# A mixer kernel on one core: the remainders and the root in the loop of the second norms

## The chip, the core and the metric

The kernel runs on one core of a Trainium2 chip. The core has five engines with an instruction queue each: TensorE (PE in the profile, with its weight loads as PEld) for matrix products, VectorE (DVE), ScalarE (ACT) and GpSimd (POOL) for elementwise work, and SyncE (SP), which issues DMAs. Each engine works through its own queue in order, and engines wait for each other by semaphores. The metric is the device time of one execution in microseconds (us): the median of several runs.

## The reference

`x` is 2048 tokens of 640 channels. Two blocks follow each other, each behind a layer norm whose scale and shift come from a conditioning vector, and each added to `x` through a gate:

```python
mod = (silu(c) @ w_mod).reshape(1, 6, 1, 640)      # sa, ca, ga, sb, cb, gb
h = layernorm(x) * (1 + ca) + sa
x = x + ga * A(h, k, v, shift_k, ssm_k, ssm_D)      # causal convolutions, gated by h
h = layernorm(x) * (1 + cb) + sb
x = x + gb * B(h, w1, b1, w2, b2)                   # token mixing

def B(x, w1, b1, w2, b2):
    h = layernorm(x)                                # a second norm, over the channels again
    u = gelu(einsum("bsd,sf->bdf", h, w1) + b1)     # F = 1728
    return (einsum("bdf,fs->bds", u, w2) + b2).transpose(0, 2, 1)
```

So between the two blocks each token's row is normalized, scaled and shifted by `1 + cb` and `sb`, and normalized once more. The change lies in the loop that does this second normalization and feeds the first product of block B.

## The kernel before

The first 300 us compute block A with Fourier matrices on TensorE. From about 300 us on, the kernel takes the 2048 tokens as 16 row tiles `j` of 128 tokens by 640 channels, two at a time: pair `pr` holds the tiles `2*pr` and `2*pr + 1`, pairs 0 to 7. `row(j)` is a tile's work place in SBUF; for tiles 4 and up it is the tile of `x` itself.

Products are made in fp32r, and so each factor is split into a half (the value rounded to fp32r) and a remainder (value minus half): three products, half by half, half by remainder and remainder by half, stand for one. `H[j]` is the pair (half, remainder) of the normalized row; `blk[f]` the pair for the weights of block `f`, of 128 columns of `w1`. The first four blocks of weights (f = 0 to 3) are multiplied inside the loop, pair by pair, and accumulate in four PSUM tiles `acc`; the other ten follow after the loop (from L882) with all 16 rows at once.

The steps for one pair:

- `x1_stats` (L665): VectorE ends the statistics of the first norm of a row (`bn_stats` L510, `bn_aggr` L668).
- `norm1` (L704): ScalarE applies the first norm to the two rows (L706).
- `second` (L708): VectorE multiplies both rows by `1 + cb` and sums them (L712), makes the negative mean (L714) and adds it and `sb` (L717); ScalarE squares each row and sums the squares into a column of `V_` (L722). The squares' own values go to the place of the later remainder and are not used.
- `root_in` (L683): the root's bias. GpSimd turns the sum of squares into a variance plus epsilon (L688) and does the same for the first norm of a pair that comes later (L691); ScalarE takes the square root of these few columns (L692).
- `root` (L694): VectorE makes the reciprocal root from it in four small operations (`newton`, L318 to L321), and the first norm's bias (L701). The result is `R_`.
- `halves` (L724): ScalarE writes the halves, `row * R_` rounded (L726).
- `rests` (L728): VectorE writes the remainders, `row * R_ - half` (L730), one instruction per row.
- `products` (L733): TensorE, 48 matmuls per pair (L433): for each row and each of the four blocks the half with the weights' half and with the weights' remainder, then for each row the remainder with the weights' half. For the last pair all three steps of a block come together.

The weights of the blocks are split by rows, four tiles `j` at a time (`split_rows`, L406): the halves on ScalarE (L409), the remainders on VectorE (L411, recorded under the helper's line L59). In the loop, `split_rows` for tiles 8 to 11 gives its halves in turn 3 and its remainders in turn 4, and for tiles 12 to 15 in turns 5 and 6.

Nothing is planned by a scheduler: the kernel asks for a manual schedule, and each engine's queue holds its instructions in the order in which the Python program writes them. That order is a matter of latency as well as of work: in the loop (L795 to L812) the queue of VectorE holds, per turn, `second` of this pair, the remainders of the pair before, in turns 4 and 6 the weight remainders, the statistics for a pair that comes later, and then the root. `root_in` comes between the statistics and the root. TensorE's products of the pair before stand behind the remainders. In turn 4, at its end, SyncE is given the load of the next block of weights (`load_w(4)`) into the tile `X`, whose old contents the weight remainders of that turn read last.

Of the kernel before, what the change touches and what calls it, by code (L numbers as in the profile page):

```python
# [10 lines left out]
F32R = mybir.dt.float32r  # L11
AF = mybir.ActivationFunctionType
ALU = mybir.AluOpType
# [36 lines left out]
def mixer_kernel(ctx: ExitStack, tc: tile.TileContext, q, k, v, shift_k, ssm_k, ssm_D, w1, b1, w2, b2, c,  # L50
# [7 lines left out]
    act, dve, pool, pe, sync = nc.scalar, nc.vector, nc.gpsimd, nc.tensor, nc.sync  # L58
    TT = lambda eng, o, a, b, op: eng.tensor_tensor(o, a, b, op=op)  # L59
    uid = [0]  # L60

    def mem(tag, n, name=None):

        return sb.tile([128, n], F32, name=name or tag, tag=tag, bufs=1)
# [4 lines left out]
    def psum(slot=None):  # L69

        uid[0] += 1
        slot = ring[uid[0] % len(ring)] if slot is None else slot
        return psp.tile([128, 1024], F32, name=f"pst_{uid[0]}", tag=f"pst{slot}", bufs=1)
# [242 lines left out]
    def newton(r, t, v, n=None):  # L316

        dve.reciprocal(r, t)  # L318
        dve.scalar_tensor_tensor(t, r, -0.5, r, op0=ALU.mult, op1=ALU.mult)
        TT(dve, t, t, v, ALU.mult)  # L320
        dve.scalar_tensor_tensor(r, t, 1.5, r, op0=ALU.add, op1=ALU.mult)  # L321
# [64 lines left out]
    def load_w(i, t=X):  # L386
        if i >= NF + NW:
            return
        if i < NF:
            t = j16(t)  # L390
            for b in range(2):
                sync.dma_start(t[64 * b:64 * b + 64],
                               dram(w1, 16 * b * F + fo(i), [[32 * F, 64], [F, 16], [1, 128]]))
            raw[i] = (t, [slice(0, 8), slice(8, 16)])
        else:
            t = f14(t)
            load_w2(t, i - NF, 0, 14)
            raw[i] = (t, [slice(0, 7), slice(7, 14)])
# [7 lines left out]
    def split_rows(r, t, blocks, hi=True, lo=True):  # L406
        j, t = slice(4 * r, 4 * r + 4), t.rearrange("p (j m) -> p j m", j=4)
        for f in blocks if hi else ():
            act.activation(blk[f][0][:, j].bitcast(F32R), t[:, :, 128 * f:128 * f + 128], AF.Copy)  # L409
        for f in blocks if lo else ():  # L410
            TT(dve, blk[f][1][:, j].bitcast(F32R), t[:, :, 128 * f:128 * f + 128], blk[f][0][:, j], ALU.subtract)  # L411
# [15 lines left out]
    def mm(ps, wh, wl, rh, rl, first, last, steps=None):  # L427

        m = wh.shape[-1]
        steps = steps or ((wh, rh), (wh, rl), (wl, rh))  # L430
        for i, (w_, r_) in enumerate(steps):
            for h in range(2):
                pe.matmul(ps[0:m, h, 0:320], w_.bitcast(F32R), r_[:, 320 * h:320 * h + 320].bitcast(F32R),  # L433
                          start=first and i == 0, stop=last and i == 2)
# [76 lines left out]
    for c in range(NC):  # L511
# [141 lines left out]
        else:  # L653
# [5 lines left out]
    H = (unit(r_z[:, 0:4096], 3) + unit(r_v, 3) + unit(mem("aux", 4096, "h_a"), 3)  # L659
         + unit(r_z[:, 3840:7680], 3))  # L660
    tmp = piece(mem("g", 1280, "t_g"), 2) + piece(T_t, 2)
    row = lambda j: tmp[j] if j < 4 else XR(j)
    acc = []

    def x1_stats(js):  # L665
        for j in js:
            x1s(NC - 1, j)()
            dve.bn_aggr(mv[:, j, :], bst[:, j])  # L668


    V_, T_, R_ = (T_kt[:, o:o + 32] for o in (1280, 1312, 1344))
# [9 lines left out]
    at = lambda t, n, j: t[:, place[n, j]:place[n, j] + 1]  # L681

    def root_in(n):  # L683

        second_, first_ = roots[n]
        o = start[n]
        if second_:
            pool.tensor_scalar(V_[:, o:o + 2], V_[:, o:o + 2], 1 / D, EPS, op0=ALU.mult, op1=ALU.add)  # L688
            o += 2
        if first_:  # L690
            pool.tensor_scalar(V_[:, o:start[n + 1]], mv[:, first_[0]:first_[-1] + 1, 1], EPS, None, op0=ALU.add)  # L691
        act.activation(T_[:, start[n]:start[n + 1]], V_[:, start[n]:start[n + 1]], AF.Sqrt)  # L692

    def root(n):  # L694

        o = slice(start[n], start[n + 1])
        newton(R_[:, o], T_[:, o], V_[:, o])
        first_ = roots[n][1]
        if first_:
            f = slice(first_[0], first_[-1] + 1)  # L700
            dve.scalar_tensor_tensor(nm1[:, f], mv[:, f, 0], -1.0, R_[:, start[n + 1] - len(first_):start[n + 1]],  # L701
                                     op0=ALU.mult, op1=ALU.mult)

    def norm1(pr):  # L704
        for j in (2 * pr, 2 * pr + 1):
            act.activation(row(j), XR(j), AF.Identity, scale=at(R_, 1, j), bias=nm1[:, j:j + 1])  # L706

    def second(pr):  # L708

        for j in (2 * pr, 2 * pr + 1):  # L710
            t = row(j)
            dve.scalar_tensor_tensor(t, t, 1.0, CB, op0=ALU.mult, op1=ALU.mult, accum_out=su[:, j:j + 1])  # L712
        n = su[:, 2 * pr:2 * pr + 2]
        dve.tensor_scalar(n, n, msb, -1 / D, op0=ALU.add, op1=ALU.mult)  # L714
        for j in (2 * pr, 2 * pr + 1):
            t = row(j)
            dve.scalar_tensor_tensor(t, t, su[:, j:j + 1], SB, op0=ALU.add, op1=ALU.add)  # L717
        for j in (2 * pr, 2 * pr + 1):
            if j == 12:
                H.extend(unit(mem("xa", 5120, "h_x"), 4))  # L720
            H[j] = H[j][:, 0:640], H[j][:, 640:1280]
            act.activation(H[j][1].bitcast(F32R), row(j), AF.Square, accum_out=at(V_, 2, j))  # L722

    def halves(pr):  # L724
        for j in (2 * pr, 2 * pr + 1):
            act.activation(H[j][0].bitcast(F32R), row(j), AF.Identity, scale=at(R_, 2, j))  # L726

    def rests(pr):  # L728
        for j in (2 * pr, 2 * pr + 1):
            dve.scalar_tensor_tensor(H[j][1].bitcast(F32R), row(j), at(R_, 2, j), H[j][0], op0=ALU.mult,  # L730
                                     op1=ALU.subtract)

    def products(pr, fs=range(4)):  # L733
        for f_ in fs:
            if f_ == len(acc):
                acc.append(psum().rearrange("p (h m) -> p h m", h=2))
        js = [(f_, j) for j in (2 * pr, 2 * pr + 1) for f_ in fs]
        if pr == 7:
            for f_, j in sorted(js):
                mm(acc[f_], blk[f_][0][:, j], blk[f_][1][:, j], *H[j], False, j == 15)  # L740
            return
        for rest in range(2):
            for f_, j in js:
                wh, wl = blk[f_][0][:, j], blk[f_][1][:, j]
                mm(acc[f_], wh, wl, *H[j], j == 0 and not rest, False, ((wh, H[j][1]),) if rest else
                   ((wh, H[j][0]), (wl, H[j][0])))
# [28 lines left out]
    halves(0)  # L775
    norm1(1)
    rests(0)
    products(0, range(3))
    x1_stats(range(4, 6))
    second(1)  # L780
    gate(NC - 1, ps, 1, dve, then=(lambda: root_in(2), lambda: root(2), lambda: halves(1), lambda: norm1(2)))
    spill(NC - 1, (1,))
    products(0, [3])
    rests(1)
    products(1)
    second(2)
# [3 lines left out]
    halves(2)  # L790
    norm1(3)
    rests(2)
    norm1(4)
    products(2)
    for pr in range(3, 8):  # L795
        second(pr)
        if pr > 3:
            rests(pr - 1)
            products(pr - 1)
        if pr in (4, 6):  # L800
            split_rows(pr // 2, X if pr == 4 else P, range(4), False, True)
        if pr < 6:
            x1_stats(range(2 * pr + 4, 2 * pr + 6))
        root_in(pr + 1)
        root(pr + 1)
        halves(pr)
        if pr < 6:
            norm1(pr + 2)
        if pr in (3, 5):
            split_rows(pr // 2 + 1, X if pr == 3 else P, range(4), True, False)  # L810
        if pr == 4:
            load_w(4)  # L812
# [258 lines left out]
def build(inputs):  # L1071
    import concourse.bacc as bacc

    nc = bacc.Bacc("TRN2", target_bir_lowering=False, num_devices=1)
    arrays, args = {}, []

    def add(name, a):
        a = np.ascontiguousarray(a)
        arrays[f"in_{name}_dram"] = a
        args.append(nc.dram_tensor(f"in_{name}_dram", a.shape, mybir.dt.from_np(a.dtype), kind="ExternalInput").ap())  # L1080

    for name in _INS:
        a = np.asarray(inputs[name])
        add(name, a.reshape(S, D) if name in ('A_q', 'A_k', 'A_v') else a)
    for name, a in _constants().items():
        add("const_" + name, a)
    args.append(nc.dram_tensor("out_0_dram", (S, D), F32, kind="ExternalOutput").ap())
    with tile.TileContext(nc) as tc:
        mixer_kernel(tc, *args)
    return nc, arrays  # L1090
# [8 lines left out]
```

## Time and profile before

| what | value |
| --- | --- |
| three runs, median | 702.24 us |
| three runs, lowest to highest | 700.96 to 708.29 us |
| the profiled execution | 707.76 us |
| its span, first to last instruction | 706.0 us |
| mean granted clock of TensorE | 0.977 |
| busy in the span: PE, DVE, ACT, POOL | 624.8, 485.5, 293.0, 128.3 us |

The profile is of one execution, with the start and the duration of each instruction. A row of the lists in order of time gives the start in us, the duration in us, the engine, the line of the kernel, the operation, output and inputs by the program's names, shapes, and the number of like instructions that the row merges; in square brackets stand the idle time of the engine ahead of it and what ended that. Where a row merges two instructions, its duration runs from the first one's start to the last one's end. L59 is a helper's line, for all two-operand operations of VectorE and GpSimd. `wb` is a tile of split weights, `h_a`, `r_z`, `r_v` and `h_x` are tiles that hold `H`, `xa` and `xb` hold the rows, `kt` holds the few columns of the root, `p` and `x` the raw weights, and `m_p`, `m_v`, `m_w` belong to the last stage.

### The profile page before, as it was taken

Reading aid. Unit: us, or ns where it says so; the run is one execution under the profiler, and the core shown is the slowest. Engines: PE = TensorE matmul, PEld = TensorE weight load, DVE = VectorE, ACT = ScalarE, POOL = GpSimd, SP = SyncE. Lnnn points to the kernel's source line nnn. Section 1 sums busy time; section 2 is a strip of 40 time slices with the busy share of each in tenths; the row PEclk is TensorE's granted clock in tenths of the full one; section 3 lists DMA queues with packets and bytes.
Section 4 is the critical chain, followed back from the end, with each engine's and each line's share of the span. In section 5 each row is a group of like instructions: output and inputs, shape, how many; then the busy total and the mean of one; then the engine's idle time right before and its main releaser. Section 6 shows DMA issues by size and latency. Waiting matters only on the chain.

```text
span 706.0 us, 20772 instructions
## 1 busy us (share of the span) xinstructions
PE 624.8 (89%) x9131; PEld 603.1 (85%) x9131; DVE 485.5 (69%) x849; ACT 293.0 (42%) x465; POOL 128.3 (18%) x147
## 2 busy tenths in 40 slices
PE   0698576898999988888799999999999998999997
PEld 0698266888998878778799999999999998999997
DVE  7779338987979539888885213211399959888986
ACT  0444263554746636456666223222335223333331
POOL 5183018512524125000110000000000340000000
PEclk9999888999999999999999999999999999999999
DMA  9977988617343524161303633353163343455411
GB/s 185 248 216 214 368 174 175 149 32 162 71 90 91 172 63 119 58 151 31 59 1 60 118 63 61 75 103 62 53 193 105 106 140 110 145 170 170 148 60 38
DMA packets 167185, 84.91 MB, mean 120 GB/s; under 512 B 89235, under 2 KB 157622, under 8 KB 167094
## 3 DMA queue, kind: packets, MB, share of 16 engines
q1 hardware_dynamic: 162546, 82.27, 46.3%
q10 hardware_dynamic: 4548, 1.31, 1.1%
q8 instruction: 71, 1.16, 0.7%
q14 instruction: 20, 0.16, 0.1%
HBM read 73.07 MB, written 10.49 MB: 118 GB/s over the span
## 4 chain that ended last, share of the span: by engine, by line
PE 64%; DVE 14%; DMA 7%; SPq 5%; ACT 5%; issue 4%; POOL 1%; ACTq 0%; DVEq 0%; POOLq 0%
PE pst L433 21%; PE pst L958 17%; PE pst L1035 7%; PE pst L219 6%; PE pst L263 4%; PE pst L234 4%; SPq L496 3%; PE pst L283 3%; DMA aux<-in_A_ssm_k_dram 2%; DVE p L59 2%; DVE tap L59 2%; DVE kt L59 2%; DMA in<-in_A_k_dram 1%; DMA w<-in_const_w_dram 1%; DMA aux<-in_w_mod_dram 1%
## 5 line engine op out<-in xcount | busy, mean ns | idle before, releaser
L234 PE MATMUL pst<-z,w 128*64 128x64 f32 x2560 | 78.8, 223 | 12.8 <-ACT z L221 5.7
L234 PEld LDWEIGHTS pst<-z,w 128*64 128x64 f32 x2560 | 76.5, 138 | 14.2 <-issue 7.2
L221 ACT ACTIVATE z<-pst 128x1024 f32<-128x1024 f32 x40 | 42.7, 1069 | 52.2 <-PE pst L219 52.1
L219 PE MATMUL pst<-v,x 128*64 128x128 f32 x640 | 40.0, 284 | 26.1 <-DVE x L59 25.2
L59 DVE TENSOR_TENSOR p<-pst,kt 128x512 f32<-128x512 f32 x80 | 51.0, 681 | 15.4 <-ACT kt L238 14.2
L219 PEld LDWEIGHTS pst<-v,x 128*64 128x64 f32 x640 | 37.3, 144 | 28.3 <-POOL t L458 23.4
L59 POOL TENSOR_TENSOR y<-p 128x256 f32<-128x256 f32 x72 | 51.1, 742 | 39.7 <-DVE p L59 39.5
L219 PE MATMUL pst<-v,p 128*64 128x128 f32 x640 | 40.1, 286 | 7.5 <-DVE aux L59 4.8
L831 ACT ACTIVATE pst<-pst,sm 128x640 f32<-128x640 f32 x14 | 10.7, 766 | 86.0 <-PE pst L433 86.0
L219 PEld LDWEIGHTS pst<-v,p 128*64 128x64 f32 x640 | 37.8, 145 | 8.5 <-DVE aux L59 5.0
L958 PE MATMUL pst<-r_z,m_w 128*128 128x320 f32 x222 | 41.6, 309 | 2.2 <-DVE m_w L59 2.2
L238 ACT ACTIVATE kt<-pst 128x512 f32<-128x512 f32 x40 | 23.9, 598 | 44.3 <-PE pst L234 27.5
L263 PEld LDWEIGHTS pst<-v,y 32*128 32x128 f32 x1280 | 38.2, 187 | 3.8 <-issue 2.6
L263 PE MATMUL pst<-v,y 32*128 32x64 f32 x1280 | 40.1, 272 | 0.7 <-ACT z L221 0.6
L946 ACT ACTIVATE m_w<-m_v 128x896 fp32r<-128x896 f32 x24 | 22.7, 951 | 35.1 <-PE pst L958 16.9
L958 PEld LDWEIGHTS pst<-r_z,m_w 128*128 128x128 f32 x222 | 34.8, 188 | 2.4 <-DVE m_w L59 2.4
L59 DVE TENSOR_TENSOR tap<-tap,kt 128x512 f32<-128x512 f32 x51 | 35.5, 696 | 1.3
L59 DVE TENSOR_TENSOR kt<-in,tap 128x512 f32<-128x512 f32 x51 | 34.9, 685 | 1.4
L59 POOL TENSOR_TENSOR m_p<-u_i,r_z 128x320 f32<-128x320 f32 x1 | 0.9, 881 | 188.7 <-issue 188.7
L283 PEld LDWEIGHTS pst<-z,v 64*64 64x64 f32 x1280 | 24.8, 159 | 9.3 <-issue 4.8
L283 PE MATMUL pst<-z,v 64*64 64x64 f32 x1280 | 26.7, 245 | 6.5 <-issue 2.9
L59 DVE TENSOR_TENSOR m_w<-m_v,m_w 128x896 fp32r<-128x896 f32 x24 | 28.1, 1173 | 2.2 <-ACT m_w L946 1.7
(280 smaller groups left out, 1441.7 us busy)
## 6 DMA issues: line engine op xcount, KB each, us to landing
x<-in_B_w_dram SPq DMA_DIRECT2D x22, 512.0 KB
m_v<-in_B_w_dram SPq DMA_DIRECT2D x15, 384.0 KB
x<-in_B_w_dram SPq DMA_DIRECT2D x14, 384.0 KB
aux<-in_A_ssm_k_dram SPq DMA_DIRECT2D x10, 512.0 KB
in<-in_A_k_dram SPq DMA_DIRECT2D x36, 128.0 KB
in<-in_A_v_dram SPq DMA_DIRECT2D x36, 128.0 KB
m_x<-xs SPq DMA_DIRECT2D x28, 160.0 KB
out_dram<-m_x SPq DMA_DIRECT2D x28, 160.0 KB
```

The lines of the kernel that those rows point to most:

```text
L59: TT = lambda eng, o, a, b, op: eng.tensor_tensor(o, a, b, op=op)
L219: pe.matmul(ps[64 * ri:64 * ri + 64, o:o + 255:2], lhs, F1[:, 128 * ri:128 * ri + 128], start=True, stop=True)
L221: evac = lambda: act.activation(Z[:, side, t], ps.rearrange("p (a k e) -> p a k e", a=4, e=2), AF.Copy)
L234: pe.matmul(ps[64 * h:64 * h + 64, o:o + 64], W2[k1 // 32][:, 2 * (k1 % 32) + ri], rhs, start=True, stop=True)
L238: act.activation(kt.rearrange("p (m i) -> p m i", i=32), pv[:, :, 1], AF.Copy)
L263: pe.matmul(pp[qd // 2][:, o:o + 64], Y[p, ri, i:i + 2].rearrange("p i k -> p (i k)"), V2[p, 64 * ri:64 * ri + 64], start=ri == 0, stop=ri ...
L283: pe.matmul(ps[64 * b:64 * b + 64, 512 * e + 64 * jj:512 * e + 64 * jj + 64], V1[p, ri, n2], T2[p, :, 32 * ri + n2], start=ri == 0, stop=r ...
L433: pe.matmul(ps[0:m, h, 0:320], w_.bitcast(F32R), r_[:, 320 * h:320 * h + 320].bitcast(F32R), start=first and i == 0, stop=last and i == 2)
L496: sync.dma_start(XH[j // 8][64 * b:64 * b + 64, j % 8], dram(q, (16 * b + j) * D, [[32 * D, 64], [1, D]]))
L946: act.activation(W[n][0].bitcast(F32R), A[p, w_], AF.Copy)
L958: pe.matmul(bank[n], w[:, i].bitcast(F32R), r.bitcast(F32R), start=i == 0 and k == 0, stop=i == 6 and k == 2)
L1035: pe.matmul(acc[s][:, h, 0:320], w[:, f_].bitcast(F32R), u[r + h].bitcast(F32R), start=f_ == 0 and k == 0, stop=f_ == NF - 1 and k == 2)
```

## The change

Three things are done, all in the loop of the second norms.

First, in `rests`, for pairs 3 to 6, the second row of the pair gets its remainder from GpSimd instead of VectorE. GpSimd multiplies the row by its reciprocal root in place, and subtracts the half in a second instruction. The first row stays with VectorE, as do both rows of the other pairs.

Second, the order within a turn of the loop: the statistics and `root_in` now come directly behind `second`, then the remainders and products of the pair before, and then the root. So the remainders stand between the root's bias and the root.

Third, the weight remainders of turns 4 and 6 come behind the root.

```diff
     def rests(pr):
-        for j in (2 * pr, 2 * pr + 1):
+
+        a, b = 2 * pr, 2 * pr + 1
+        if pr in (3, 4, 5, 6):
+            pool.tensor_scalar(row(b), row(b), at(R_, 2, b), None, op0=ALU.mult)
+            TT(pool, H[b][1].bitcast(F32R), row(b), H[b][0], ALU.subtract)
+        for j in (a,) if pr in (3, 4, 5, 6) else (a, b):
             dve.scalar_tensor_tensor(H[j][1].bitcast(F32R), row(j), at(R_, 2, j), H[j][0], op0=ALU.mult,
                                      op1=ALU.subtract)
...
     for pr in range(3, 8):
         second(pr)
+        if pr < 6:
+            x1_stats(range(2 * pr + 4, 2 * pr + 6))
+        root_in(pr + 1)
         if pr > 3:
             rests(pr - 1)
             products(pr - 1)
+        root(pr + 1)
         if pr in (4, 6):
             split_rows(pr // 2, X if pr == 4 else P, range(4), False, True)
-        if pr < 6:
-            x1_stats(range(2 * pr + 4, 2 * pr + 6))
-        root_in(pr + 1)
-        root(pr + 1)
         halves(pr)
```

## The prediction

> **What bounds the kernel now.** I read the page first, then the table by stretches, then the engines' lists of instructions in order of time for the stretch of the loop.
>
> ```profile
> span 706.0 us, 20772 instructions
> 336.00:376.00 40.00, 35.41 (x227) 34.62 (x227) 33.37 (x79) 26.10 (x48) 3.51 (x6) 0.96 0.14 27
> 376.00:540.00 164.00, 163.11 (x1112) 162.85 (x1111) 62.95 (x101) 53.58 (x83) 0.00 (x0) 1.00 0.42 91
> ```
>
> The columns are the stretch, its length, the busy time of PE, PEld, DVE, ACT and POOL, PE's granted clock, the share of DMA and GB/s. From 376 on PE is busy 163.11 of 164 us: what the loop gains or loses at its end moves everything behind it, and nothing there gives it back. The loop (336 to 379) is another matter: PE and DVE are both idle at times.
>
> ```profile
> 319.59 2.62 PE L433 MATMUL pst<-r_z,wb 128*128 128x320 f32 x16 [0.25 <-ACT r_z L726]
> ...
> 329.40 7.32 PE L433 MATMUL pst<-r_v,wb 128*128 128x320 f32 x48 [2.47 <-ACT r_v L726]
> 338.00 7.33 PE L433 MATMUL pst<-h_a,wb 128*128 128x320 f32 x48 [1.28 <-ACT h_a L726]
> 348.09 3.87 PE L433 MATMUL pst<-h_a,wb 128*128 128x320 f32 x16 [2.76 <-ACT h_a L726]
> ...
> 364.56 14.33 PE L433 MATMUL pst<-h_x,wb 128*128 128x320 f32 x96 [0.55 <-ACT h_x L726]
> 379.79 2.92 PE L433 MATMUL pst<-r_z,wb0b 128*128 128x320 f32 x18 [0.89 <-DVE u_x L59]
> ```
>
> A pair needs 48 matmuls, 7.3 us, or 0.149 us each (14.33 / 96). PE waits for the normalized half (L726) three times: 1.28, 2.76 and 0.55 us. After 2.76 us of idling 16 matmuls take 3.87 us where 2.62 was the usual: 1.25 us more at a lower clock; after 2.47 us there is no such loss. All that the change can win is therefore 2.76 + 0.55 + 1.25 = 4.6 us, since the first wait lies ahead of what is changed.
>
> What L726 waits for is the root, and the root stands in DVE's order behind everything else of its turn:
>
> ```profile
> 339.07 1.68 DVE L717 SCALAR_TENSOR_TENSOR xb<-xb,sm,kt 128x640 f32<-128x640 f32 x2
> 340.67 1.67 DVE L730 SCALAR_TENSOR_TENSOR h_a<-xa,kt,h_a 128x640 fp32r<-128x640 f32 x2
> 342.27 2.49 DVE L59 TENSOR_TENSOR wb<-x,wb 128x512 fp32r<-128x512 f32 x4
> 344.68 0.28 DVE L510 BATCH_NORM_STATS2 sm<-xb 128x6 f32<-128x128 f32 x1
> ...
> 346.33 0.18 DVE L318 RECIPROCAL kt<-kt 128x4 f32<-128x4 f32 x1 [0.57 <-ACT kt L692]
> ...
> 347.01 0.16 DVE L321 SCALAR_TENSOR_TENSOR kt<-kt 128x4 f32<-128x4 f32 x1
> ...
> 347.29 0.82 DVE L712 SCALAR_TENSOR_TENSOR xb<-xb,kt 128x640 f32<-128x640 f32 x1
> ...
> 350.75 0.88 DVE L730 SCALAR_TENSOR_TENSOR h_a<-xb,kt,h_a 128x640 fp32r<-128x640 f32 x1
> ```
>
> Here `second` is 3.46 us (347.29 to 350.75), the two remainders 1.6, the weight remainders 2.41 (342.27 to 344.68), the statistics some 1.05.
>
> **The change part by part.** The halves of pairs 3, 4, 5, 6 and 7 begin at these times, and the squares (L722) end so; with them stand the second step of the last `second`, the load that follows the weight remainders, and the first use of its tile:
>
> ```profile
> 337.12 1.55 ACT L726 ACTIVATE h_a<-xa,kt 128x640 fp32r<-128x640 f32 x2 [0.91 <-DVE kt L321]
> 343.63 0.19 ACT L722 ACTIVATION_READ_ACCUMULATOR r_z<-xb 128x1 f32 x1
> 347.21 0.83 ACT L726 ACTIVATE h_a<-xb,kt 128x640 fp32r<-128x640 f32 x1 [0.91 <-DVE kt L321]
> 354.88 1.55 ACT L726 ACTIVATE r_z<-xb,kt 128x640 fp32r<-128x640 f32 x2 [0.90 <-DVE kt L321]
> 361.39 0.19 ACT L722 ACTIVATION_READ_ACCUMULATOR h_x<-xb 128x1 f32 x1
> 363.68 1.55 ACT L726 ACTIVATE h_x<-xb,kt 128x640 fp32r<-128x640 f32 x2 [0.89 <-DVE kt L321]
> 365.44 1.68 DVE L717 SCALAR_TENSOR_TENSOR xb<-xb,sm,kt 128x640 f32<-128x640 f32 x2
> 367.80 0.18 ACT L722 ACTIVATION_READ_ACCUMULATOR h_x<-xb 128x1 f32 x1
> 369.89 1.55 ACT L726 ACTIVATE h_x<-xb,kt 128x640 fp32r<-128x640 f32 x2 [0.89 <-DVE kt L321]
> 344.78 1.33 SPq L392 DMA_DIRECT2D x<-in_B_w_dram  x2
> 373.65 2.01 ACT L422 ACTIVATE wb0b<-x 128x1024 fp32r<-128x1024 f32 x2 [2.21 <-PE pst L433]
> ```
>
> Removed from DVE: one L730 in each of four turns, 4 x 0.8 = 3.2 us. Added on POOL: four multiplications and four subtractions of 128x640. Moved: `root_in` ahead of the remainders (POOL's and ACT's queues), the weight remainders (DVE) behind the root.
>
> *POOL's two passes.* The subtraction by rows:
>
> ```profile
> 11.15 1.26 POOL L59 TENSOR_TENSOR t<-t 128x512 f32<-128x512 f32 x1
> 557.50 0.88 POOL L59 TENSOR_TENSOR m_p<-u_i,r_z 128x320 f32<-128x320 f32 x1 [188.74 <-issue]
> 21.58 1.09 POOL L458 TENSOR_SCALAR t<-rows 128x256 f32<-128x256 f32 x1
> 23.33 0.63 DVE L458 TENSOR_SCALAR tap<-rows 128x256 f32<-128x256 f32 x1
> 301.97 0.82 DVE L370 TENSOR_SCALAR kt<-pst 128x640 f32<-128x640 f32 x1
> ```
>
> From 0.88 (320) and 1.26 (512) the line gives 1.5 to 1.55 us at 640; I take 1.55. The multiplication isn't in the trace at this size. Its own operation took 1.09 us for 256 elements read at a step of four, 2.7 us at 640 if length alone counts. But DVE took 0.63 us on that same pattern and 0.82 for 640 elements in a row; by that ratio POOL needs 1.09 x 0.82 / 0.63 = 1.4. I take 1.5, nearest to this and to POOL's own subtraction, with 0.8 (DVE's 640) and 2.7 as ends. The Trainium skill (GPSIMD Engine Reference, section 4.1 Engine selection) calls one-input work on GpSimd roughly line-rate, which no row here shows; 640 elements at its 1.2 GHz would be an estimate of 0.53 us and a sum 3.9 us lower.
>
> *What they collide with.* POOL starts its pair right behind the root's bias, and the root's own small DVE operations come in the same moment. What happens when both engines read SBUF:
>
> ```profile
> 556.70 0.49 DVE L59 TENSOR_TENSOR m_p<-m_p 128x320 f32<-128x320 f32 x1
> ...
> 557.68 1.04 DVE L59 TENSOR_TENSOR m_p<-m_p 128x320 f32<-128x320 f32 x1
> ...
> 335.49 0.19 POOL L688 TENSOR_SCALAR kt<-kt 128x2 f32<-128x2 f32 x1 [8.13 <-ACT h_a L722]
> 335.76 0.22 POOL L691 TENSOR_SCALAR kt<-sm 128x2 f32<-128x2 f32 x1
> 343.90 0.91 POOL L688 TENSOR_SCALAR kt<-kt 128x2 f32<-128x2 f32 x1 [7.92 <-ACT r_z L722]
> ```
>
> The same DVE operation takes 0.49 us alone and 1.04 when started inside POOL's 557.50 to 558.38: it ends 0.34 us behind POOL, so it was held until POOL was done. The other way round, L688 takes 0.91 instead of 0.19 beside the weight remainders (342.27 to 344.76). One waits for the other's whole instruction. The Trainium skill (SBUF — State Buffer, section Who interferes with whom) has this as an exclusive lock between a GpSimd instruction that reads SBUF and a VectorE instruction with two SBUF inputs; these rows agree, and by it the change puts its POOL work in the worst place.
>
> Of the root's four DVE operations the last three (L319, L59, L321) read two operands from SBUF. Unhindered, from L688 to the halves are 337.12 - 335.49 = 1.63 us (0.27 less where a root has no L691). With POOL's pair: it starts 0.54 us behind L688, 1.5 us of multiplication hold L319; L319 slips through between; the subtraction (0.1 + 1.55) holds L59; then L59, L321 and the handing over, 0.4. In sum 4.1 us, or 3.83 without L691: **2.5 us more on the chain in each turn**, where 0.8 us of DVE work left it.
>
> *The sum, turn by turn.* Turn 4: the squares end at 343.82 as before (ACT's order is unchanged), L688 at 343.90 meets an idle DVE; halves at 343.9 + 4.1 = 348.0 (before 347.21). PE, through 40 of its 48 matmuls at 338.00 + 5.96 = 343.96, waits for row 7's remainder, which POOL has at 343.90 + 0.54 + 1.5 + 0.1 + 1.55 = 347.6. Turn 5: weight remainders 348.1 to 350.5, `second` to 354.0, squares 0.86 later (as in turn 7: 367.98, against L717's 365.44 + 1.68), L688 at 355.0; L691 then waits some 0.6 for DVE's remainder behind the statistics; halves at 359.7 (354.88). Turn 6: ACT sets the pace; halves to the squares' end is 361.58 - 354.88 = 6.70, so 366.4, halves 0.1 + 3.83 later at 370.3 (363.68). Turn 7: 370.4 + 2.41 + 3.46 + 0.86 = 377.1, halves 3.9 later at 381.0 (369.89). Then row 14's half (0.83) and its remainder on DVE (0.85) at 382.7, PE having done four matmuls of the last 48; 44 x 0.149 = 6.56 more end at 389.3. Before it was 364.56 + 14.33 = 378.89: **10.4 us later**.
>
> The weight remainders cost the same 2.41 twice, only later; they feed products whose half comes 0.83 behind the same root, and are hidden by it but for some tenths. `load_w(4)`, behind them in SP's order, goes out some 6 us later than now (344.78); its tile is first read at 373.65 now, and about 10 us later then, so this is free. Nothing else stands in POOL's queue.
>
> In the profiled execution (707.76 us, 1.76 outside its span) this makes 718.2. That one lies 5.5 above the median of the three runs, 702.24; on the median: **712.6 us**. The sum moves by 4 us for each us of the multiplication.
>
> **The rivals.**
> (a) Multiplication short, 0.8 us, at DVE's pace: 10.4 - 2.8 = +7.6, 709.8. For it: the inputs are in a row. Against: all POOL rows are slower per element than DVE's. The line-rate of the Trainium skill's page named above would put it at 708.7.
> (b) Multiplication long, 2.7: +15.2, 717.4. For it: POOL's only large row of this operation.
> (c) **Not slower:** DVE's small operations aren't held, only long ones are; place: L319 to L321 beside POOL's pair. Then the halves come 1.63 (or 1.36) behind L688: 345.5, 354.0, 362.2; L688 of turn 7 at 369.1. PE then waits only for POOL's remainder of row 13 (369.1 + 0.27 + 3.15 = 372.5); 8 + 48 matmuls more end at 380.9: +2.0, 704.2. Against: the 557.68 row. The point from which it decides: a pair of passes under 1.1 us would come out even, under that faster, at most by the 4.6 us above (697.6). A single 320-element pass already took 0.88.
> (d) The order is not what the code says: the program keeps its own written order, so this hardly can be.
>
> **How the numbers follow.** Forecast 0.45, (a) 0.20, (b) 0.17, (c) 0.13, the faster end of (c) 0.03, (d) 0.02. A lower clock after the longer PE waits adds up to 1.25 us. The range runs from 706 (between (a) and (c)) to 720 ((b), the clock, and a us or two of runs); below it lie (c) and its end. About 1%, 7 us, is what a measurement here tells from none: the three runs spread from 700.96 to 708.29. Slower by more: the forecast, (b), and two thirds of (a), 0.75. Faster by more than 1% is beyond the 4.6 us, left at 0.02 for what I don't see.
>
> **What would show it.** L319 or L59 of the root drawn out to over a us, each ending 0.2 us behind a POOL pass; four POOL multiplications, whose length settles (a) and (b); L688 in turn 4 back at 0.19; PE waiting for POOL's remainder in place of L726, with up to four waits of 2 to 4 us; halves at about 348, 360, 370 and 381; everything from 379 on shifted and unchanged in itself. I'd be wrong if the root's operations keep their 0.16 us beside POOL, or POOL's pair takes well under 2 us.

## The result, and the profile after

The changed kernel's median is 712.61 us over 20 runs (706.44 to 716.88); the kernel before, run beside it, has 704.84 over 20 runs (700.07 to 708.71). The ratio is 1.0102, with a 95% interval from 1.008 to 1.0124: the change makes the kernel slower by about 1%, some 7 us.

The profiled execution of the changed kernel has, of all things, the shorter span, 704.7 us against 706.0: it was the fastest of the 20. So the span is the wrong thing to compare. I cut both traces at two instructions that both kernels have: the first matmul of pair 3 in the loop, and the first matmul of weight block 4, behind the loop. The columns are those of the prediction's table by stretches. Before:

```profile
338.00:379.79 41.79, 37.59 (x241) 36.80 (x241) 33.91 (x76) 28.20 (x50) 3.51 (x6) 0.96 0.16 30
379.79:706.00 326.21, 320.00 (x2178) 319.48 (x2178) 199.04 (x297) 101.74 (x147) 14.28 (x12) 1.00 0.41 107
```

After:

```profile
330.20:378.47 48.27, 38.10 (x240) 36.79 (x241) 36.64 (x72) 28.37 (x50) 15.96 (x14) 0.96 0.13 27
378.47:704.70 326.23, 320.00 (x2178) 319.47 (x2178) 198.46 (x297) 101.80 (x147) 15.14 (x12) 1.00 0.41 106
```

Behind the loop both take 326.2 us. The loop takes 48.27 in place of 41.79: **6.48 us more**, 0.92% of 704.84, within the interval. What lies ahead of the loop is the same code in both; it took 338.00 us in the one execution and 330.20 in the other, and from 330 to 343 over all traces of this document. From here on the loop's stretch is the measure. It is read from one execution of each kernel; the ratio of the medians stands beside it.

In the loop, TensorE now waits for GpSimd where it waited for the normalized halves:

```profile
330.20 6.15 PE L433 MATMUL pst<-h_a,wb 128*128 128x320 f32 x40 [1.27 <-ACT h_a L726]
340.13 5.32 PE L433 MATMUL pst<-h_a,wb 128*128 128x320 f32 x24 [3.79 <-POOL h_a L59]
...
351.03 7.33 PE L433 MATMUL pst<-r_z,wb 128*128 128x320 f32 x48 [2.04 <-POOL r_z L59]
359.69 1.44 PE L433 MATMUL pst<-r_z,wb 128*128 128x320 f32 x8 [1.33 <-POOL r_z L59]
...
369.05 8.47 PE L433 MATMUL pst<-h_x,wb 128*128 128x320 f32 x56 [2.05 <-POOL h_x L59]
378.47 2.91 PE L433 MATMUL pst<-r_z,wb0b 128*128 128x320 f32 x18 [0.95 <-DVE u_x L59]
```

That was foreseen. What VectorE does beside GpSimd was not (lists in order of time, GpSimd's first; L732 is GpSimd's multiplication, its L59 the subtraction, L735 VectorE's remainder):

```profile
336.11 0.19 POOL L688 TENSOR_SCALAR kt<-kt 128x2 f32<-128x2 f32 x1 [7.93 <-ACT r_z L722]
...
336.57 1.89 POOL L732 TENSOR_SCALAR xa<-xa,kt 128x640 f32<-128x640 f32 x1
338.55 1.53 POOL L59 TENSOR_TENSOR h_a<-xa,h_a 128x640 fp32r<-128x640 f32 x1
```

```profile
337.08 0.30 DVE L319 SCALAR_TENSOR_TENSOR kt<-kt 128x4 f32<-128x4 f32 x1
337.49 0.16 DVE L59 TENSOR_TENSOR kt<-kt 128x4 f32<-128x4 f32 x1
...
337.96 3.87 DVE L59 TENSOR_TENSOR wb<-x,wb 128x512 fp32r<-128x512 f32 x4
...
356.13 0.43 DVE L319 SCALAR_TENSOR_TENSOR kt<-kt 128x2 f32<-128x2 f32 x1
...
356.94 3.84 DVE L59 TENSOR_TENSOR wb<-p,wb 128x512 fp32r<-128x512 f32 x4
```

The root is hardly held: its second operation takes 0.30 to 0.43 us in place of 0.16, its third 0.16 as before, both inside the 1.89 us of the multiplication. But the root is through so early that the weight remainders, now right behind it, meet the subtraction: 3.87 and 3.84 us in place of 2.49. In turn 5, which has no weight remainders, it meets the second norm (L712), as shown further down.

### The profile page after: what moved, and what is told of

Same layout as the page of the kernel before. It is cut to its first block, busy times and chain, and to the rows that moved or that the text cites. A ratio compares the mean times of both kernels' runs of the same rounds, so it can differ in the third digit from the quotient of the medians.

```text
span 704.7 us, 20783 instructions
## 1 busy us (share of the span) xinstructions
PE 624.6 (89%) x9131; PEld 600.4 (85%) x9131; DVE 487.9 (69%) x845; ACT 293.7 (42%) x465; POOL 141.7 (20%) x155
## 4 chain that ended last, share of the span: by engine, by line
PE 62%; DVE 16%; SPq 6%; DMA 5%; issue 5%; ACT 5%; POOL 1%; ACTq 0%; DVEq 0%; POOLq 0%
PE pst L433 20%; PE pst L963 17%; PE pst L1040 7%; PE pst L219 6%; PE pst L263 4%; PE pst L234 4%; SPq L496 3%; PE pst L283 2%; DVE tap L59 2%; DVE p L59 2%; DVE kt L59 2%; SPq L152 1%; DVE aux L59 1%; DMA aux<-in_w_mod_dram 1%; DMA w<-in_const_w_dram 1%
## 5 line engine op out<-in xcount | busy, mean ns | idle before, releaser
L59 DVE TENSOR_TENSOR p<-pst,kt 128x512 f32<-128x512 f32 x80 | 50.8, 680 | 13.1 <-ACT kt L238 10.6
L59 POOL TENSOR_TENSOR y<-p 128x256 f32<-128x256 f32 x72 | 51.2, 745 | 36.8 <-DVE p L59 36.6
L59 POOL TENSOR_TENSOR m_p<-u_i,r_z 128x320 f32<-128x320 f32 x1 | 0.9, 884 | 187.3 <-DVE m_p L59 187.3
L59 DVE TENSOR_TENSOR tap<-tap,kt 128x512 f32<-128x512 f32 x51 | 35.5, 696 | 1.3
L59 DVE TENSOR_TENSOR kt<-in,tap 128x512 f32<-128x512 f32 x51 | 34.9, 685 | 1.4
L272 ACT ACTIVATE z<-pst 128x512 f32<-128x512 f32 x38 | 20.8, 641 | 20.3 <-PE pst L263 20.3
```

## The experiments

My theory after the traces (A): the loss is that GpSimd's remainder is late and its subtraction holds VectorE's weight remainders. The rival (B): the new order costs, whoever makes the remainders, because weight remainders behind the root push the next second norm back. The predicted theory, a held root, is tested by the kernels that leave out one of GpSimd's two passes. All edits below are against the changed kernel.

### The new order without GpSimd

```diff
-        if pr in (3, 4, 5, 6):
+        if pr in ():
...
-        for j in (a,) if pr in (3, 4, 5, 6) else (a, b):
+        for j in (a, b):
```

> Left out of the change: GpSimd's part; both remainders stay on VectorE, the new order of the turn and the late weight remainders are kept. The measure is the loop's stretch, from pair 3's first matmul to block 4's first: 41.79 us before, 48.27 with the whole change. Theory A (GpSimd's remainder comes late to TensorE and its subtraction holds the weight remainders): most of the 6.48 goes with GpSimd; the order alone leaves row 8's remainder behind the weight remainders and the next second norm, so TensorE waits for it in turn 5; by adding the rows, 43.0 us, +1.3. Theory B (the new order itself costs, because the weight remainders behind the root push the next second norm): 46 us or more.

```profile
338.51 7.33 PE L433 MATMUL pst<-h_a,wb 128*128 128x320 f32 x48 [1.27 <-ACT h_a L726]
346.92 2.62 PE L433 MATMUL pst<-h_a,wb 128*128 128x320 f32 x16 [1.08 <-ACT h_a L726]
...
353.88 1.45 PE L433 MATMUL pst<-h_a,wb 128*128 128x320 f32 x8 [2.00 <-DVE h_a L735]
...
382.26 2.91 PE L433 MATMUL pst<-r_z,wb0b 128*128 128x320 f32 x18 [0.89 <-DVE u_x L59]
```

The stretch is 382.26 - 338.51 = 43.75 us, +1.96; the ratio of times 1.0033 (0.9997 to 1.0069). Pair 4's first matmul comes 8.41 us behind pair 3's, where it was 10.09, so the root is earlier, and the lower clock of before is gone (16 matmuls in 2.62 us, where they took 3.87). All of it and more is lost again: weight remainders, second norm and statistics stand ahead of row 8's remainder on VectorE, and TensorE waits 2.00 us for it. By the stretches theory A has the larger part of the 6.48 and B some of it; the interval of the times, which includes 1, does not show B by itself.

### GpSimd's remainder in the old order

```diff
     for pr in range(3, 8):
         second(pr)
-        if pr < 6:
-            x1_stats(range(2 * pr + 4, 2 * pr + 6))
-        root_in(pr + 1)
         if pr > 3:
             rests(pr - 1)
             products(pr - 1)
-        root(pr + 1)
         if pr in (4, 6):
             split_rows(pr // 2, X if pr == 4 else P, range(4), False, True)
+        if pr < 6:
+            x1_stats(range(2 * pr + 4, 2 * pr + 6))
+        root_in(pr + 1)
+        root(pr + 1)
```

> Left out of the change: the new order. GpSimd makes the second row's remainder, but everything else stands in the order of before, so its pair starts as soon as the turn's halves are there, ahead of the root's bias in GpSimd's queue. Theory A: the pair (1.9 + 1.5 us) is done by about 342, before TensorE is through 40 matmuls, and runs beside the second norm, where its subtraction holds one VectorE operation for up to 1.5 us and takes back the 0.8 us saved; stretch 40.8 to 42.0 us, no wait of TensorE for GpSimd. Theory B: as before, 41.8, less 0.8 a turn at best. A theory that GpSimd as such costs: 46 us or more.

```profile
332.98 4.97 PE L433 MATMUL pst<-h_a,wb 128*128 128x320 f32 x32 [1.28 <-ACT h_a L726]
...
343.95 4.64 PE L433 MATMUL pst<-h_a,wb 128*128 128x320 f32 x16 [3.07 <-ACT h_a L726]
...
378.19 2.91 PE L433 MATMUL pst<-r_z,wb0b 128*128 128x320 f32 x18 [0.89 <-DVE u_x L59]
```

45.21 us, +3.42, ratio 1.0054 (1.0022 to 1.0086). My expectation of 40.8 to 42.0 was wrong, though TensorE never waits for GpSimd here. The remainder is early enough; what it costs stands on VectorE:

```profile
334.06 2.02 DVE L717 SCALAR_TENSOR_TENSOR xb<-xb,sm,kt 128x640 f32<-128x640 f32 x2
336.00 2.20 DVE L735 SCALAR_TENSOR_TENSOR h_a<-xa,kt,h_a 128x640 fp32r<-128x640 f32 x1
...
344.75 0.78 DVE L714 TENSOR_SCALAR sm<-sm 128x2 f32<-128x2 f32 x1
```

Beside GpSimd's pair, L717 takes 2.02 in place of 1.68, L714 0.78 in place of 0.23, and the remainder left to VectorE 2.2 in place of 0.88. To save 0.8 us of VectorE work in a turn, VectorE is held for 1.6 to 1.9. The halves come later (343.07, which is 10.97 us behind pair 3's, where it was 10.09), and TensorE waits longer for them (3.07 us) and then runs at a lower clock: 16 matmuls in 4.64 us at a granted 0.50, where before they took 3.87 and at full clock 2.62.

### The weight remainders ahead of the root again

```diff
-        root(pr + 1)
         if pr in (4, 6):
             split_rows(pr // 2, X if pr == 4 else P, range(4), False, True)
+        root(pr + 1)
```

> The change with its third part undone: the weight remainders again ahead of the root (between the root's bias and the root). Theory A: in turns 4 and 6 they run while the squares are made, before GpSimd's subtraction, and take 2.49 us instead of 3.85; the wait for GpSimd's remainder stays; stretch 44.2 to 45.5 us. Theory B puts all of the loss on the place of the weight remainders: back to 42 or less. If the root were held by GpSimd, the stretch would stay at 48.

```profile
336.43 6.11 PE L433 MATMUL pst<-h_a,wb 128*128 128x320 f32 x40
347.01 5.84 PE L433 MATMUL pst<-h_a,wb 128*128 128x320 f32 x24 [4.46 <-POOL h_a L59]
...
382.02 2.91 PE L433 MATMUL pst<-r_z,wb0b 128*128 128x320 f32 x18 [0.95 <-DVE u_x L59]
```

```profile
340.81 2.49 DVE L59 TENSOR_TENSOR wb<-x,wb 128x512 fp32r<-128x512 f32 x4
...
345.48 2.15 DVE L712 SCALAR_TENSOR_TENSOR xb<-xb,kt 128x640 f32<-128x640 f32 x1
```

45.59 us, 2.68 less than with the whole change and still 3.80 more than before; ratio 1.0076 (1.0035 to 1.0117); I had expected 44.2 to 45.5. The weight remainders are back at 2.49, but the subtraction now holds an operation of the next second norm, L712, with 2.15 us in place of 0.82. The hold moves; it doesn't go.

### The same order, all on VectorE

```diff
-        if pr in (3, 4, 5, 6):
+        if pr in ():
...
-        root(pr + 1)
         if pr in (4, 6):
             split_rows(pr // 2, X if pr == 4 else P, range(4), False, True)
+        root(pr + 1)
```

> No GpSimd work; the statistics and the root's bias directly behind the second norm, then both remainders and the weight remainders on VectorE, then the root. Theory A (VectorE must be kept busy while the squares and the root's bias are made, and not be held by GpSimd): in turn 4 the 1.6 + 2.5 us of VectorE work fill the 3 us until the root's bias is there; by adding the rows 40.0 to 41.2 us for the loop's stretch, 0.6 to 1.8 less than before, some 0.2% of the time, and no drawn-out operation anywhere. If the early place of the root's bias itself cost, as with the order alone (43.75), it would stay at 43 or more.

```profile
334.33 7.33 PE L433 MATMUL pst<-h_a,wb 128*128 128x320 f32 x48 [1.27 <-ACT h_a L726]
344.41 4.15 PE L433 MATMUL pst<-h_a,wb 128*128 128x320 f32 x16 [2.74 <-ACT h_a L726]
...
375.83 2.91 PE L433 MATMUL pst<-r_z,wb0b 128*128 128x320 f32 x18 [0.89 <-DVE u_x L59]
```

```profile
340.24 1.86 POOL L688 TENSOR_SCALAR kt<-kt 128x2 f32<-128x2 f32 x1 [7.92 <-ACT r_z L722]
```

41.50 us, 0.29 less than before; ratio 0.9989 (0.9965 to 1.0012), no difference that can be measured. I had expected 40.0 to 41.2. Here the hold works against GpSimd: the root's bias, two numbers per partition, takes 1.86 us in place of 0.19 and ends at 342.10, just behind VectorE's weight remainders (339.55 to 342.04). With this kernel the stretches make a table, in us:

| | weight remainders ahead of the root | behind it |
| --- | --- | --- |
| both remainders on VectorE | 41.50 | 43.75 |
| one remainder on GpSimd | 45.59 | 48.27 (the change) |

From the 41.79 of before, the earlier place of statistics and bias gives -0.29, the weight remainders behind the root +2.25, and GpSimd +4.52, or +4.09 in the other column. By way of the 43.75, the three sum up to the 6.48: -0.29, +2.25 and +4.52. What the place of the weight remainders does can be followed in the halves (L726) of the two kernels without GpSimd's remainder: where the weight remainders stand behind the root, the halves of turns 5 and 7 come 9.80 and 8.62 us behind those of the turn before, and 7.39 and 6.20 where they stand ahead of it. So each pushes the next second norm back by its 2.4 us; in turns 4 and 6 some of that is won back.

### One of GpSimd's two passes left out

The first of these kernels leaves the second row's remainder unmade, the second subtracts from a row that is not scaled. Both, and the next kernel, were timed once, so they have a stretch and no interval.

```diff
 # no_subtraction
-            TT(pool, H[b][1].bitcast(F32R), row(b), H[b][0], ALU.subtract)
 # no_multiplication
-            pool.tensor_scalar(row(b), row(b), at(R_, 2, b), None, op0=ALU.mult)
```

> The whole change without GpSimd's subtraction: the second row's remainder is not made (the squares that lie in its place are multiplied instead), the multiplication stays. Theory A: the weight remainders go back from 3.85 to 2.49 us, TensorE no longer waits 3.8, 2.0, 1.3 and 2.0 us for GpSimd's subtraction but at most for other things; stretch about 44 us. The root's second operation (0.30 to 0.43 us) stays as long as with the change, since it is the multiplication that runs beside it. Theory B: 48, since the order is the same.

```profile
336.16 7.33 PE L433 MATMUL pst<-h_a,wb 128*128 128x320 f32 x48 [1.27 <-ACT h_a L726]
...
379.78 2.91 PE L433 MATMUL pst<-r_z,wb0b 128*128 128x320 f32 x18 [0.95 <-DVE u_x L59]
```

```profile
343.91 2.50 DVE L59 TENSOR_TENSOR wb<-x,wb 128x512 fp32r<-128x512 f32 x4
```

43.62 us without the subtraction, as expected, and as good as with no GpSimd work at all (43.75): the multiplication alone is nearly free, and leaving out the subtraction saves 4.65.

> The whole change without GpSimd's multiplication, so that the subtraction (of the unscaled row) starts where the multiplication did, beside the root. Theory A (a GpSimd operation holds VectorE as long as it reads; the subtraction reads all through its 1.53 us): the root's second operation, 0.30 to 0.43 us with the multiplication beside it, is drawn out to 1.2 to 1.4 us, ending with the subtraction; the weight remainders are back at 2.5 us; the stretch 46 to 47 us. If the root's small operations slip through whatever GpSimd does, they stay at 0.2 to 0.4 and the stretch comes out near 43.8, as without the subtraction.

```profile
340.15 6.15 PE L433 MATMUL pst<-h_a,wb 128*128 128x320 f32 x40 [1.27 <-ACT h_a L726]
...
386.79 2.91 PE L433 MATMUL pst<-r_z,wb0b 128*128 128x320 f32 x18 [0.96 <-DVE u_x L59]
```

```profile
346.52 1.53 POOL L59 TENSOR_TENSOR h_a<-xa,h_a 128x640 fp32r<-128x640 f32 x1
```

```profile
346.82 0.18 DVE L318 RECIPROCAL kt<-kt 128x4 f32<-128x4 f32 x1 [2.17 <-ACT kt L692]
347.04 1.03 DVE L319 SCALAR_TENSOR_TENSOR kt<-kt 128x4 f32<-128x4 f32 x1
```

46.64 us. With the subtraction beside it, the root is held as the prediction had it: L319 takes 1.03 us and ends at 348.07, GpSimd at 348.05; the four turns have 1.03 to 1.18, a little under the 1.2 to 1.4 that I had expected. The root's first operation, the reciprocal (L318) with one input, keeps its 0.18 us beside the subtraction. So it depends on the pass how long the root is held. The two passes don't simply add up: the subtraction alone costs 2.89 us (46.64 against 43.75), and the multiplication ahead of it, which makes it 1.9 us later, 1.63 more.

### Half a multiplication

```diff
-            pool.tensor_scalar(row(b), row(b), at(R_, 2, b), None, op0=ALU.mult)
+            pool.tensor_scalar(row(b)[:, 0:320], row(b)[:, 0:320], at(R_, 2, b), None, op0=ALU.mult)
```

> The whole change with GpSimd's multiplication over the first 320 of 640 columns only (the others are not scaled). Theory A (the multiplication reads for about 0.65 of its 1.89 us, and holds VectorE that long): it takes about 1.0 us, reads for 0.33, and the root's second operation, which asks 0.5 us behind its start, is back at 0.16 us in all four turns. If the hold is a fixed time per GpSimd instruction, that operation stays at 0.30 to 0.43. The subtraction comes 0.9 earlier; stretch 45.5 to 47.5 us.

```profile
349.34 1.09 POOL L732 TENSOR_SCALAR xa<-xa,kt 128x320 f32<-128x320 f32 x1
```

```profile
349.84 0.16 DVE L319 SCALAR_TENSOR_TENSOR kt<-kt 128x4 f32<-128x4 f32 x1
```

With the whole row, L319 ended 0.81, 0.80, 0.80 and 0.80 us behind the multiplication's start in the changed kernel's four turns (first and third: 337.38 - 336.57, and 356.56 - 355.76). With half the row it takes 0.16 or 0.17 us in the four turns, although it starts 0.37 to 0.51 us into a multiplication of 1.09. The hold is longer with more columns and shorter than the instruction. That it lasts as long as GpSimd reads is the explanation that I find likely; the reads themselves are in no trace. The stretch is 46.89 us (from 342.97 to 389.86), in the range expected.

### TensorE's late products put off

```diff
+    late = []
+
...
         for rest in range(2):
-            for f_, j in js:
+            todo = js
+            if rest and pr > 2:
+                todo = late + [q for q in js if q[1] % 2 == 0]
+                late[:] = [q for q in js if q[1] % 2]
+            for f_, j in todo:
```

For the last pair the products put off come ahead of row 15's, block by block.

> The whole change, and TensorE's products with GpSimd's remainder put off by one pair, behind the next pair's halves, so that TensorE has other work while GpSimd ends. Theory A1 (the loss is VectorE's: its work is held and its chain to the next halves is longer): the waits of 3.8, 2.0, 1.3 and 2.0 us for GpSimd go, but TensorE waits for halves and for VectorE's last remainders in their place; stretch 47.3 to 48.3 us. Theory A2 (the loss is TensorE's waiting for GpSimd's remainder): 44.5 us or less.

```profile
332.21 6.15 PE L433 MATMUL pst<-h_a,wb 128*128 128x320 f32 x40
...
371.80 10.97 PE L433 MATMUL pst<-h_x,wb 128*128 128x320 f32 x54 [1.50 <-DVE h_x L735]
382.61 2.81 PE L433 MATMUL pst<-r_z,wb0b 128*128 128x320 f32 x18
```

```profile
371.80:382.61 10.81, 10.81 (x54) 10.81 (x55) 4.52 (x6) 6.03 (x8) 0.00 (x0) 0.71 0.19 44
```

50.40 us, more than either theory gave; ratio 1.0107 (1.0068 to 1.0146), like the change itself. None of TensorE's waits is for GpSimd any more, and nothing is won: it waits for halves and for VectorE's remainders (1.50 us for the last). The 2.1 us beyond the change can be put down to the clock: the last 54 matmuls take 10.97 us at a granted 0.71, where 54 x 0.149 = 8.05. Without this it would be an estimated 47.5, in A1's range. The halves (L726) come 8.55, 19.38, 27.75 and 37.53 us behind pair 3's, as good as in the changed kernel (8.56, 19.36, 27.74 and 37.47): VectorE's chain is as late without TensorE's waits for GpSimd as with them. So A2, that TensorE's waiting for GpSimd is itself the loss, falls.

## Why the prediction was right, and where it wasn't

**The time.** 712.6 was forecast and 712.61 measured, but that closeness is luck: the forecast was 10.4 us on the 702.24 of three runs, and measured are 6.5 (the stretch), 7.2 (the ratio) or 7.8 us (the medians) on a median of 704.84, so that a sum too large and a base too low cancel. The side and the mechanism's place (GpSimd's pair beside work of VectorE that reads SBUF) were right; the sum was too large by 4 us.

**The step that failed** is "2.5 us more on the chain in each turn". I took it from a subtraction (the 557.68 row) and gave it to both passes. The multiplication holds the root for 0.14 to 0.27 us, not for its whole 1.89; the root is through before the subtraction starts. Counted from pair 3's halves, the later halves were forecast at 10.9, 22.6, 33.2 and 43.9 us (348.0, 359.7, 370.3 and 381.0 less 337.12) and came at 8.56, 19.36, 27.74 and 37.47:

```profile
329.32 1.55 ACT L726 ACTIVATE h_a<-xa,kt 128x640 fp32r<-128x640 f32 x2 [0.91 <-DVE kt L321]
337.88 0.83 ACT L726 ACTIVATE h_a<-xb,kt 128x640 fp32r<-128x640 f32 x1 [1.05 <-DVE kt L321]
...
348.68 1.55 ACT L726 ACTIVATE r_z<-xb,kt 128x640 fp32r<-128x640 f32 x2 [1.05 <-DVE kt L321]
357.06 1.55 ACT L726 ACTIVATE h_x<-xb,kt 128x640 fp32r<-128x640 f32 x2 [1.16 <-DVE kt L321]
366.79 1.55 ACT L726 ACTIVATE h_x<-xb,kt 128x640 fp32r<-128x640 f32 x2 [1.16 <-DVE kt L321]
```

Against the 10.09, 17.76, 26.56 and 32.77 of before, the first halves are even earlier. The loss falls in turns 5 and 7, which follow the weight remainders: 10.80 and 9.73 us from halves to halves, in place of 7.67 and 6.21. So at the last halves the forecast was 6.4 us too late. Behind them it was too early: 8.3 us were forecast up to the end of the loop's matmuls (389.3 less 381.0) and 10.73 came, since GpSimd's subtraction ended only at 369.00 and 56 matmuls stood behind it. In the sum a part of the first error is hidden by the second.

**What took its place.** The subtraction holds what stands behind the root, in each of the four turns: 1.4 us on the weight remainders in turns 4 and 6 (3.87 and 3.84, against 2.49), 1.3 on L712 in turn 5 (2.15, against 0.82), and 1.1 on the remainders of the last pair (2.82, against 1.68). After:

```profile
349.51 2.15 DVE L712 SCALAR_TENSOR_TENSOR xb<-xb,kt 128x640 f32<-128x640 f32 x1
...
367.65 2.82 DVE L735 SCALAR_TENSOR_TENSOR h_x<-xb,kt,h_x 128x640 fp32r<-128x640 f32 x2 [0.90 <-ACT h_x L726]
```

I had written that the weight remainders "cost the same 2.41 twice, only later", and that is how they stand on the chain of turns 5 and 7 in the sum. They don't cost the same, and the later place costs by itself 2.25 us (43.75 against 41.50), since the next second norm stands behind them.

**Rival (c)** had it right that the root's operations go on beside the multiplication, and gave +2.0. Its reason, that small operations aren't held, doesn't stand: beside the subtraction L319 takes 1.03 us. It lacked the hold on the weight remainders. Neither case of mine had the mixture, a nearly free root and a held successor.

**Terms.** Subtraction: 1.55 forecast, 1.53 measured. Multiplication: 1.5 forecast, 1.89 measured, between the 1.4 by VectorE's ratio and the 2.7 by length alone, and nearer to the first. By the forecast's own 4 us for each us of it, the 0.39 us more would have made the sum 1.6 us larger still. L688 of turn 4 at 0.19: as forecast. TensorE's four waits for GpSimd, 2 to 4 us: 3.79, 2.04, 1.33 and 2.05, one of them shorter. Behind the loop nothing changed: 326.21 and 326.23. (Four of the eight traces of the experiments have 327.7 there, with a granted clock of 0.98 in place of 1.00 between 500 and 600 us: those with only the new order, with the weight remainders ahead, without the subtraction and with half a multiplication.) That the change could win at most 4.6 us was never tested: no kernel here won more than 0.29.

**The two rules of the Trainium skill.** That the lock is held for the whole instruction (the Trainium skill, SBUF — State Buffer, Who interferes with whom) fits the subtraction and not the multiplication, beside which VectorE's operation of 0.16 us ends 0.80 us after the start. Line-rate for one input (the Trainium skill, GPSIMD Engine Reference, 4.1 Engine selection) isn't what the runs show: 1.09 us for 320 and 1.89 for 640 elements are 2.5 ns for each further element.

## What to carry to other kernels

Work moved to GpSimd isn't free of VectorE: a two-input pass there held VectorE's two-input operations on SBUF until its end, so that 0.8 us saved in a turn cost VectorE 1.4 to 1.9. When you move work off an engine, look at what will stand beside it at the moment it really runs, and then at what runs there if your own answer about the first collision is wrong. And when spans of single executions differ by more than the change can do, cut both traces at instructions that they share.

## What was not expected of the hardware

GpSimd's one-input pass over 640 columns takes 1.89 us, but a VectorE operation with two SBUF inputs that starts 0.37 to 0.51 us into it ends 0.80 us behind its start; with 320 columns it isn't held at all there. A subtraction of two inputs holds to its end (348.07 against 348.05). Also held was a VectorE operation that isn't one with two large inputs: L714 of the kernel with the old order, 128x2, with 0.78 us in place of 0.23, ended 0.82 us behind the start of the multiplication beside it:

```profile
344.71 1.89 POOL L732 TENSOR_SCALAR xb<-xb,kt 128x640 f32<-128x640 f32 x1 [2.79 <-DVE xb L712]
```

And a burst of VectorE operations that follow each other without a gap can keep a small GpSimd operation out to its end: 1.86 us for L688. It doesn't always: with the weight remainders ahead of the root and GpSimd's remainder kept, L688 of turn 4 began at 342.29 and was through after 0.46 us, while the weight remainders went on until 343.30. Which of the two comes about is open.

The length of a single wait didn't decide TensorE's clock either. Before, a wait of 2.47 us was followed by 48 matmuls in the usual 7.3 us. In the trace with the weight remainders ahead, 2.25 us were followed by 48 in 8.81 at a granted 0.81, and in that of the late products 2.41 us by 16 in 4.98 at 0.50.
